# Tile shapes on TensorE and the planned order in a two-layer memory-attention kernel: 64x64 tiles for all 64-row products, 32-column quarters where they fit, an order from a slot table

## The chip, the core and the metric

The kernel runs on one core of a Trainium2 chip. The metric is the device time of one execution in microseconds; lower is better. The kernel before took 1589.48 us, the median of five runs between 1587.12 and 1594.11.

Engines are called as the profile calls them: PE is TensorE's matmul, PEld its weight load, DVE is VectorE, ACT ScalarE, POOL GpSimd, SP the queue that issues most DMAs. A matmul `MM(out, lhsT, rhs)` loads `lhsT` (rows x columns) into the array and streams `rhs` through it; "128x32" below is a tile of 128 rows and 32 columns of the array, and four such tiles can work at once, as can two of 64x128 or four of 64x64.

## The reference, cut to what matters

```
x = A_x                                   # 2048 positions, 448 wide, bf16
x = x + A(layernorm(x), mem0, ...)        # layer 0: attention with a recurrent memory
x = x + B(layernorm(x), ...)              # gated feed-forward, width 1792
x = x + A(layernorm(x), mem0, ...)        # layer 1, same weights
x = x + B(layernorm(x), ...)

def A(x, mem, Wq, Wk, Wv, Wo):            # 16 heads of 256
    for s in range(64):                   # segments of 32 positions
        h = concat([mem, x[segment s]])   # 8 + 32 = 40 rows
        q, k, v = h Wq, h Wk, h Wv
        p = softmax(masked(q k^T / 16))
        o = (p v) Wo
        mem, out[segment s] = o[:8], o[8:]

def B(x):  return (relu(x Wg) * (x Wu)) Wd
```

The memory of segment s+1 comes out of segment s, so the 64 segments of a layer are a chain.

## The kernel before, in words

**Folded weights.** A setup of some 67 us loads the weights and multiplies each head's Wq with its Wk (into `M`, and `M3` for the last 64 of the 448 rows) and Wv with Wo (into `N`). The 448-wide contraction is cut into three chunks of 128 rows (`c` or `kt` 0 to 2) and one of 64 rows (3). `NO = 56` output chunks of 128 stand for 16 heads of 448.

**Steps.** The two layers run in one loop of 68 steps; in step t, layer 0 works on segment t and layer 1 on segment t-4 (`LAG`). Up to step 3 there is only layer 0, in the last four only layer 1; between them a product of 40 rows a layer streams 80 columns. One step queues these operations (method, and tile shape on PE):

- `t_block` (L821): T = M^T h, 56 chunks in three blocks. A 64-row part (`first`) of pairs of chunks, two 64x128 tiles at once, then `rest`: three 128x128 matmuls of 80 columns a chunk. The last block has one unit and no pairs; it uses 128 rows throughout. Copies to `TTm` and `TTs` follow.
- `s_mem` (L890) and its softmax on DVE and ACT; `p_t_mem` (L961), a transpose; `u_mem` (L977), U = h^T p for the memory rows, in 64x128 tiles for three chunks and 64x64 for the last; `un_mem` (L990), U N in 128x32 tiles, four at once, 14 deep; its result is split into `hi` and `lo`; `m_t` (L1008) and, in the next step, `m_nat` (L1028) pick the new memory rows from them. This is the chain from step to step.
- `s_seg` (L912) and its softmax, `seg_pt` (L951, a transposing DMA from `Ps` to `PTs`), `u_seg` (L1059): the same for the 32 positions, off the chain; U products in 64x128 tiles for c < 3, 64x64 for c = 3.
- every second step: `un` (L1101), value sums over 56 chunks of 448 columns, for even p in 128x64 tiles, two at once, for odd p in 128x128; `ln_b`; `b_layer` (L1134), gate and up in a 64-row part (64x128 tiles, two at once) and a 128-row part, then down (`b_down` from L1166); `ln_a` of a later pair.

**The order.** No engine runs in the order above. `_Order.run` (L273) is a planner on the host: a list scheduler with a cost for each operation (`mm` L736, `dcost` L712, `acost`, `hop`), which at each turn takes, for the engine that can start earliest, the ready operation of highest priority. The priority is the longest path to the end plus a bias by the operation's name and step (`BIAS`, `bias_keys`). An operation has a `mode`, its tile shape (0: 128x128, 1: 64x128, 2: 128x32, 3: 64x64, 6: 128x64); `mode2` is the shape that it ends in. A change of mode costs 95 in the planner, and `stay` is a bonus for keeping it. Eight PSUM banks (`POOLS`) are handed out in planned order. Every engine then runs its list strictly in that order and waits on semaphores. All matmuls are issued by `_Sched.pe` (L117; the matmul itself is line 128 in the profile), all copies by `cp` (L725).

## Time and profile before

| What | Value |
|---|---|
| median of five runs | 1589.48 us (1587.12 to 1594.11) |
| the profiled execution | 1587.12 us, of which the span from first to last instruction is 1585.2 |
| granted TensorE clock, mean | 0.996 |
| matmuls, weight loads | 30146 each |
| DVE, ACT instructions | 2303, 2649 |
| DMA share over the span | 12.5% of 16 engines on the main queue |
| instruction fetch for the largest queue | 3.88 MB |

How to read it: the page's part 1 gives busy time by engine. Matmuls are pipelined, so the length of one (200 ns for 80 columns) says when its result is out, and the distance between two starts says what it costs. Timeline rows merge like instructions that stand next to each other: start, time to the last end, engine, line, operation, output and inputs, shape (rows*columns of the weights, then partitions x moving elements) and count; in brackets the idle time of the engine before the row and what ended it. Waits rows have engine, line and what it waited for, with total us, times, and the longest.

### The profile page before, as it was taken

The page shows a single profiled execution, that of the slowest core. Times are in us where ns is not written, and L with a number is a line of the kernel's source. Part 1 is how long each engine was busy: PE and PEld are TensorE (multiplying, and loading weights), DVE is VectorE, ACT ScalarE, POOL GpSimd, SP SyncE. Part 2 cuts the span into 40 slices and gives each one's busy share as a digit, 9 for nine tenths or more (in the row PEclk, how much of TensorE's full clock was granted, in tenths as well). Part 3 has the DMA queues.
Part 4 walks back from the last instruction along what each step waited for, and adds up shares of the span by engine and source line. Part 5 has one row for each costly group of instructions (what it writes and reads, how often), then busy time and mean ns, then how long its engine had stood idle before and what let it go on. Part 6 is the DMA issues. An engine that isn't in the chain of part 4 may idle for free.

```text
span 1585.2 us, 67069 instructions
## 1 busy us (share of the span) xinstructions
PE 1512.4 (95%) x30146; PEld 1082.9 (68%) x30146; DVE 869.7 (55%) x2303; ACT 861.5 (54%) x2649; POOL 111.1 (7%) x259
## 2 busy tenths in 40 slices
PE   5989999999999999999999999999999999999998
PEld 2456677767766776676767767776777677666775
DVE  6544546565554646555564655555465655556464
ACT  5735655555554565655555555555455465545443
POOL 4000000000000000000000000000000000000000
PEclk9999999999999999999999999999999999999999
DMA  9830000001000101010010001001000000000010
GB/s 216 224 80 18 18 9 19 19 18 15 15 19 11 23 15 19 19 15 15 18 20 11 19 19 16 17 16 19 11 19 19 19 15 18 14 14 19 13 21 13
DMA packets 128653, 45.04 MB, mean 28 GB/s; under 512 B 117480, under 2 KB 127472, under 8 KB 128368
## 3 DMA queue, kind: packets, MB, share of 16 engines
q1 hardware_dynamic: 128016, 40.52, 12.5%
q8 instruction: 237, 3.88, 1.1%
q14 instruction: 48, 0.39, 0.1%
q10 hardware_dynamic: 352, 0.24, 0.1%
HBM read 10.33 MB, written 1.84 MB: 8 GB/s over the span
## 4 chain that ended last, share of the span: by engine, by line
PE 86%; DVE 7%; DMA 3%; ACT 2%; issue 2%; POOL 0%; DVEq 0%; ACTq 0%; POOLq 0%
PE b L128 86%; DMA PTs<-Ps 2%; DVE lo L1006 1%; ACT hi L1005 1%; DVE stat L762 1%; DVE big L732 1%; DVE xn L769 1%; DVE ys L1185 1%; DVE XA L1177 1%; DVE UTm L732 1%; ACT stat L764 0%; ACT big L731 0%; DVE hT L732 0%; DMA xAT<-xn 0%; DVE seln L602 0%
## 5 line engine op out<-in xcount | busy, mean ns | idle before, releaser
L128 PE MATMUL b<-hT,Mw 128*128 128x80 bf16 (+1 forms) x11424 | 440.4, 200 | 9.3 <-DVE hT L732 5.5
L128 PEld LDWEIGHTS b<-hT,Mw 128*128 128x128 bf16 x11424 | 419.0, 100 | 34.5 <-DVE hT L732 14.9
L731 ACT ACTIVATE TTs<-b 128x320 bf16<-128x320 f32 (+5 forms) x698 | 297.3, 426 | 29.2 <-PE b L128 28.2
L128 PE MATMUL b<-Nw,big 128*64 128x448 bf16 (+1 forms) x1936 | 308.5, 355 | 0.2 <-ACT big L731 0.2
L731 ACT ACTIVATE TTm<-b 128x80 bf16<-128x80 f32 (+5 forms) x698 | 162.6, 233 | 159.3 <-PE b L128 156.2
L128 PE MATMUL b<-xBT,big 128*128 128x128 bf16 (+3 forms) x3920 | 199.4, 214 | 1.0 <-DMA xBT<-xn 0.6
L128 PEld LDWEIGHTS b<-Nw,big 128*64 128x64 bf16 (+1 forms) x1936 | 127.3, 104 | 106.0 <-issue 11.5
L128 PE MATMUL b<-Nw,UTm 128*32 128x448 bf16 x3752 | 191.0, 355 | 6.0 <-DVE UTm L732 4.9
L128 PEld LDWEIGHTS b<-xBT,big 128*128 128x128 bf16 (+1 forms) x3920 | 177.5, 97 | 19.0 <-ACT PTm L731 10.0
L128 PEld LDWEIGHTS b<-Nw,UTm 128*32 128x32 bf16 x3752 | 97.6, 97 | 95.9 <-ACT UTm L731 14.1
L731 ACT ACTIVATE big<-b 128x512 bf16<-128x512 f32 (+1 forms) x259 | 128.9, 567 | 35.4 <-PE b L128 35.1
L128 PE MATMUL b<-hT,M 64*128 64x80 bf16 (+3 forms) x3808 | 140.7, 197 | 2.7 <-DVE M L732 1.0
L732 DVE CAST TTm<-b 64x64 bf16<-64x64 f32 (+4 forms) x186 | 40.1, 216 | 163.9 <-PE b L128 161.8
L732 POOL COPY hK<-xn 32x448 bf16<-32x448 bf16 x136 | 75.0, 551 | 717.6 <-DVE xn L769 711.1
L128 PEld LDWEIGHTS b<-hT,M 64*128 64x128 bf16 (+1 forms) x3808 | 105.6, 97 | 22.5 <-DVE hT L732 7.7
L731 ACT ACTIVATE UTm<-b 128x448 bf16<-128x448 f32 (+2 forms) x129 | 70.3, 546 | 65.4 <-PE b L128 65.0
L732 DVE CAST UTm<-b 128x448 bf16<-128x448 f32 (+2 forms) x122 | 73.3, 621 | 56.0 <-PE b L128 54.0
L732 DVE CAST TTs<-b 64x256 bf16<-64x256 f32 (+4 forms) x186 | 73.2, 394 | 55.2 <-PE b L128 55.1
L1161 ACT ACTIVATE gT<-b 128x512 bf16<-128x512 f32 (+2 forms) x128 | 69.0, 539 | 53.4 <-PE b L128 53.3
L1162 DVE TENSOR_TENSOR hB<-gT,b 128x512 bf16<-128x512 bf16 (+2 forms) x128 | 78.4, 613 | 34.7 <-PE b L128 29.4
L128 PE MATMUL b<-big,hB 128*128 128x448 bf16 (+1 forms) x490 | 97.1, 354 | 0.0
L904 DVE TENSOR_REDUCE stat<-b 128x2 f32<-128x80 f32 (+1 forms) x67 | 15.7, 234 | 145.8 <-PE b L128 145.8
(111 smaller groups left out, 1615.1 us busy)
## 6 DMA issues: line engine op xcount, KB each, us to landing
big<-in_A_Wo_dram SPq DMA_DIRECT2D x3, 896.0 KB, 5.7
out_dram<-ys SPq DMA_DIRECT2D x32, 56.0 KB, 1.9
big<-in_B_W_down_dram SPq DMA_DIRECT2D x1, 1568.0 KB, 6.9
XA<-in_A_x_dram SPq DMA_DIRECT2D x28, 56.0 KB, 2.2
big<-in_B_W_up_dram SPq DMA_DIRECT2D x1, 1344.0 KB, 6.8
big<-in_B_W_gate_dram SPq DMA_DIRECT2D x1, 1344.0 KB, 11.3
PTs<-Ps SPq DMA_TRANSPOSE x67, 2.5
Nw<-in_A_Wo_dram SPq DMA_DIRECT2D x1, 896.0 KB, 6.4
```

What stands on the lines that cost most here:

```text
L128: ins = E.matmul(out, lhsT=lhsT, rhs=rhs, **kw)
L731: return E.activation(out(), src(), ACT.Copy)
L732: return E.tensor_copy(out(), src())
L762: S.dve(lambda E: E.bn_stats(st[:, so:so + 6], x), D, rd, [(key, 0)])
L769: S.dve(lambda E, a=a, b=b, src=src: E.tensor_scalar(S.xn[:, i, a:b], src, st[:, so + 6:so + 7], st[:, so + 8:so + 9], op0=ALU.subtract, o ...
L904: S.dve(lambda E: E.tensor_reduce(st[:, 32:32 + nl], src(), AX.X, ALU.max), n, C.res(), [("sm", 0)])
L1005: S.act(lambda E: E.activation(S.hi[:, :], C.b()[:, 0:D], ACT.Copy), D, C.res(), [("hi",)])
L1006: S.dve(lambda E: E.tensor_tensor(S.lo[:, :], C.b()[:, 0:D], S.hi[:, :], ALU.subtract), D, C.res() + [("hi",)], [("lo",)])
L1161: S.act(lambda E, g=g, R=R, n=n: E.activation(S.gT[:, g, 0:n], R[0].b()[:, 0:n], ACT.Relu), n, R[0].res(), [("gT", g)])
L1162: S.dve(lambda E, g=g, R=R, n=n, fcs=fcs: E.tensor_tensor(S.hB[:, fcs[0]:fcs[-1] + 1, 0:w], S.gT[:, g, 0:n].rearrange("p (a b) -> p a b", ...
L1177: S.dve(lambda E: E.tensor_tensor(S.XA[64:128, q % 4, :], O.b()[0:64, 0:D], S.XB[0:64, p % 2, :], ALU.add), D, O.res(half=(0,)) + xb, [("X ...
L1185: S.dve(lambda E: E.tensor_tensor(S.ys[64:128, p % 2, :], O.b()[64:128, 0:D], S.XB[64:128, p % 2, :], ALU.add), D, O.res(half=(1,)) + xb, ...
```

## The change

1. **64x64 tiles.** In `t_block` and `b_layer`, `first` issues four matmuls of 64 rows and 64 columns where it had two of 64 rows and 128 columns. `u_mms` does the same for c < 3. All these operations have mode 3; mode 1 is gone, and so is `mode2`.
2. **Quarters.** `un` for even p and the 64-row `b_down` issue 128x32 tiles (mode 2) in place of 128x64. `m_t`, `m_nat`, `un` for odd p and the full `b_down` get `alt=2`: when the planner has mode 2 at that point, each of their matmuls is issued as four of 32 columns (`quarters`), else as before.
3. **The order.** `BIAS` is replaced, and for PE operations of the steps a table `SLOT` (172 entries, by name, number and t % 4) with `PERIOD` gives the key; other operations get theirs from their successors. Choosing on PE, the planner adds 95 to the start of an operation in another mode; the window for choosing is 108 where it was 60.
4. **Costs in the planner** for DVE, ACT and POOL operations and for hops between engines are changed; they alter no instruction, only the order.

```diff
+PERIOD = 86000.0
+SLOT = {
+    "t_block0f.0@0": 15263, "t_block0r.0@0": 9584, "t_block0r.1@0": -78435, "t_block0r.2@0": -78572,
...
 def bias_keys(o):
     if not o.cat:
-        return [""]
-    phase = "a" if o.t < LAG else "z" if o.t >= NSEG else str(o.t % 4)
-    return [o.cat + ("" if o.kind == "pe" else "+"), o.cat + "@" + phase]
+        return []
+    if o.kind != "pe":
+        return [o.cat + o.sub + "+"]
+    return [o.cat + "@a"] if o.t < LAG else [o.cat + "@z"] if o.t >= NSEG else []
...
-        return 90.0 if b == "pe" else 35.0
+        return 35.0 if b != "pe" else 140.0 if a == "act" else 95.0
...
+            if o.slot in SLOT:
+                o.key = SLOT[o.slot] + PERIOD * (o.t // 4)
+            else:
+                lat = self.LAT[o.eng[0]] if o.lat is None else o.lat
+                o.key = min([q.key - (0.0 if o.kind == q.kind == "pe" else lat + 60.0) for q in o.succs], default=1e9) - min(o.cost.values())
+            o.key += sum(BIAS.get(k, 0.0) for k in bias_keys(o))
+            o.prio = -o.key
...
-                t0 = min(x[0] for x in lst)
-                lim = max(f, t0) + (60.0 if e == "pe" else 40.0)
+                sw = {o: 95.0 if e == "pe" and mode not in (o.mode, o.alt) else 0.0 for _, o in lst}
+                lim = max(f, min(x + sw[o] for x, o in lst)) + (BIAS.get("win", 60.0) if e == "pe" else 40.0)
...
             if e == "pe":
-                mode = o.mode2
+                if o.alt is not None and o.alt == mode:
+                    o.mode = mode
+                if o.mode != mode:
+                    c += 95.0
+                mode = o.mode
...
-                self.sc.pe(o.fn(), res(o.rd), res(o.wr))
+                mms = o.fn()
+                self.sc.pe(_Kernel.quarters(mms) if o.alt is not None and o.mode == 2 else mms, res(o.rd), res(o.wr))
...
-        return 150.0 + n / 0.96 / speed
+        return 156.0 + n / 0.96 if speed == 1 else 280.0 + 0.26 * n
...
+    def quarters(mms):
+
+        return [(out[32 * i:32 * i + 32], lhsT[:, 32 * i:32 * i + 32], rhs, kw) for out, lhsT, rhs, kw in mms for i in range(4)]
...
 # t_block, first():
-                    for x in (a, b):
+                    for o, x in ((0, a), (0, b), (1, a), (1, b)):
                         c, u0, m = units[x]
                         side, slot = S.PLACE[16 * c + u0 + j]
-                        h = slice(64 * side, 64 * side + 64)
-                        out.append(MM(R[x].b()[:, j * n:j * n + n], S.M3[h, slot, :], mov(3, h), start=(j == 0), stop=False))
+                        h, g = slice(64 * side, 64 * side + 64), slice(64 * o, 64 * o + 64)
+                        out.append(MM(R[x].b()[g, j * n:j * n + n], S.M3[h, slot, g], mov(3, h), start=(j == 0), stop=False))
...
 # u_mms:
-            return [MM(ps[:, 0:16 * w], S.hK[r, pp, s, c * 128:c * 128 + 128], PT[r, 0:16 * w], start=True, stop=True)]
+            return [MM(ps[64 * o:64 * o + 64, 0:16 * w], S.hK[r, pp, s, c * 128 + 64 * o:c * 128 + 64 * o + 64], PT[r, 0:16 * w], start=True, stop=True)
+                    for o in range(2)]
...
 # un, even p:
-                S.mm(lambda k=k: [MM(O.b()[64 * (o % 2):64 * (o % 2) + 64, 0:D], S.U[:, o, 32 * u[0]:32 * u[0] + 64], S.N[:, o, :], start=(o < 2), stop=(o >= NO - 2))
-                                  for o in range(k, k + 4)], 2 * S.pitch(D), [("U", i, k // 16) for i in u], O.res(), mode=6)
+                S.mm(lambda k=k: [MM(O.b()[64 * (o % 2) + 32 * i:64 * (o % 2) + 32 * i + 32, 0:D], S.U[:, o, 32 * u[i]:32 * u[i] + 32], S.N[:, o, :],
+                                     start=(o < 2), stop=(o >= NO - 2)) for o in range(k, k + 4) for i in range(2)],
+                     2 * S.pitch(D), [("U", i, k // 16) for i in u], O.res(), mode=2)
...
 # b_layer, first():
-                return [MM(R[x].b()[:, i * w:i * w + w], S.W3[64 * x:64 * x + 64, fc * 128:fc * 128 + 128], S.xBT[64 * x:64 * x + 64, 3, r],
-                           start=(i == 0), stop=False) for _, fcs, R in units for i, fc in enumerate(fcs) for x in range(2)]
+                return [MM(R[x].b()[64 * o:64 * o + 64, i * w:i * w + w], S.W3[64 * x:64 * x + 64, fc * 128 + 64 * o:fc * 128 + 64 * o + 64],
+                           S.xBT[64 * x:64 * x + 64, 3, r], start=(i == 0), stop=False)
+                        for _, fcs, R in units for i, fc in enumerate(fcs) for o in range(2) for x in range(2)]
```

Not shown: `m_t`, `m_nat`, `un` and `b_down` calls with `alt=2`, the 128x32 form of the short `b_down`, and names (`sub`) that tell operations apart in the table.

## The prediction

> **What bounds the kernel now.** First the page's busy times: which engine is full?

> ```profile
> span 1585.2 us, 67069 instructions
> PE 1512.4 (95%) x30146; PEld 1082.9 (68%) x30146; DVE 869.7 (55%) x2303; ACT 861.5 (54%) x2649; POOL 111.1 (7%) x259
> PE 86%; DVE 7%; DMA 3%; ACT 2%; issue 2%; POOL 0%; DVEq 0%; ACTq 0%; POOLq 0%
> ```

> PE is full, and the chain that ended last is 86% PE. DVE and ACT are half empty, so the change counts by what it does to PE. A busy share of 95% doesn't say what PE does with the time, so I took the timeline. The score products of TTm show that the program repeats every four steps (both layers of two positions): 90.8 us, such as this stretch (PE, PEld, DVE, ACT, POOL busy, clock, DMA):

> ```profile
> 607.10:697.90 90.80, 88.63 (x1778) 64.67 (x1776) 50.41 (x129) 50.43 (x155) 5.74 (x14) 1.00 0.10 17
> ```

> Then PE's own timeline inside one step (start, length, tile shape rows*columns, moving elements, count):

> ```profile
> 717.52 0.30 PE L128 MATMUL b<-PTs,hK 40*64 40x256 bf16 x4 [0.72 <-DVE big L732]
> 717.75 0.57 PE L128 MATMUL b<-Nw,big 128*64 128x448 bf16 x4
> 718.25 0.18 PE L128 MATMUL b<-selm,hi 128*128 128x16 bf16 x1
> ...
> 718.93 2.08 PE L128 MATMUL b<-Nw,big 128*64 128x448 bf16 x20
> 721.06 0.71 PE L128 MATMUL b<-hT,M 64*128 64x80 bf16 x30
> 721.70 0.28 PE L128 MATMUL b<-hT,Mw 128*128 128x80 bf16 x3
> ...
> 722.57 3.39 PE L128 MATMUL b<-hT,Mw 128*128 128x80 bf16 x90
> 725.89 0.53 PE L128 MATMUL b<-hT,M 64*128 64x80 bf16 x20
> 726.36 0.32 PE L128 MATMUL b<-hT,Mw 128*128 128x80 bf16 x4
> ```

> Read start to start, not lengths, which overlap. 30 matmuls of 64x80 (15 pairs, two row halves at once) take 721.70-721.06 = 0.64 us; 20 (10 pairs) take 0.47. The difference, 0.17 for five pairs, is 0.035 us a pair; what remains, 0.64 - 15x0.036 = 0.10 us, is paid once, where the tile shape changes. A full 128x80 matmul costs the same 0.036 (90 in 3.32 us, one change among them). **So a change of tile shape costs PE about 0.1 us**, and nothing else in these rows is slack.

> One period's pure streaming, from pitches read this way (0.036 for 80 columns, 0.056 for 128, 0.189 for 448, 0.216 for 512, 0.025 for 40 or fewer): T 4x(174+25)x0.036 = 28.7; scores 4x40x0.025 = 4.0; memory chain (transpose, U, selection, m_nat) 3.3; un_mem 4x14x0.19 = 10.6; U of the segment 3.0; value sums (28 pairs + 56)x0.189 = 15.9; gate/up 2x(14+84)x0.056 = 11.0; down 2x14x0.189 = 5.3. Sum 81.8 us. Over eight periods (607.1 to 1333.8) the timeline has 448 changes of shape, 56 a period; at 0.096 on average 5.4 us. The remaining 90.8-81.8-5.4 = **3.6 us are waits**, of which the waits view names 18 us in eight periods (waits over 150 ns only):

> ```profile
> PE b L128 <- DVE big L732: 5.7, 8, 0.7
> PE b L128 <- DVE lo L1006: 4.1, 7, 0.7
> PE b L128 <- DVE hT L732: 3.3, 8, 0.7
> PE b L128 <- DVE UTm L732: 2.6, 8, 0.3
> PE b L128 <- DMA PTs<-Ps: 2.1, 6, 0.7
> PE b L128 <- ACT big L731: 0.4, 2, 0.2
> ```

> All are short, eight in eight periods: the same places each time, set by the planned order.

> **The change, part by part.**

> *64x64 tiles* (T's 64-row parts, U, gate/up first). A pair becomes four matmuls of half the columns that stream together. Streaming saves nothing: 25 groups of 80 moving columns replace 25 pairs. What goes is a shape: U products change from 64x128 to 64x64 within themselves (48 times in eight periods), and all 64-row work can now stand side by side.

> The unknown is a long train of 64x64 groups; the trace has only single groups of four. Such a group at 717.52 took 0.23 us for 256 columns (0.107 of streaming), 0.02 to 0.03 above the 0.1 of a change; two pairs of 128*64 at 717.75 took 0.50 against 2x0.189+0.10, again 0.02. That is a 64-column load with nothing to hide it, about 25 ns. It isn't paid per pair: the ten pairs at 718.93 took 2.13 against 1.99 + 0.02, and PE waited for hT besides. Bounds for a group of 80 columns: 36 ns (the load lies under the previous group's 33 ns of streaming) to 61 (each pays its load). I take 36, plus 0.02 once a run. Removal of the cover is rival 3.

> [...] The rows above show 25 ns, and the measurement decides.

> Also the instructions: T gains 50 matmuls and 50 loads a step, U 12, gate/up 14, the even value sums 14. In T's groups eight instructions must start in 36 ns. The fastest lasting row is 30 matmuls of 64x40 at 101.41, 15 pairs in 0.48 us with a change: 25 ns for four instructions, 6.2 each, so a group would be 50. Bounds 36 to 50; single groups of eight begin within 13 ns, so I take 36 and keep 50 as rival 2.

> *32-column quarters.* Even value sums and the short down become 128x32 always; odd value sums, down, m_t and m_nat take that shape where PE is already in it. Pitch: 56 of 128x32 (un_mem) stand at 14 groups in 2.66 us, 0.19, the full matmul's 0.189. Cost nothing, up to 0.001 a group (0.1 us a period). m_t's eight matmuls of 16 moving columns become eight groups; 25 ns each, as now, to 50 (eight instructions at the 6.2 above), 0.8 us a period; I take 25, since 16 columns stream in less than the 40 of that row. Gain: changes between 128x64, 128x32 and 128x128.

> *Changes left.* Relabelling the shapes along the present order, 56 a period become 47. The new planner counts the change in when an operation is ready and keys each PE operation apart, so the order is new. The dependences of a step need T's first part (64), its rest (128), the second pair (64, 128), scores and transpose (128), U (64), un_mem to m_nat (32): six changes, 24 a period, if fillers fit. They can: behind un_mem wait hi, lo and hT, and value sums and down (5.3 us a step) are of its shape; behind the scores, the softmax waits for gate/up's main part and the segment's scores, all 128. Bounds 24 to 47; eight PSUM banks, six of them taken by T's first block, won't let every filler in. I take 30: 30x0.1 = 3.0, with 12 exposed 64-column loads (7 now) included.

> *Waits.* The new order moves copies on DVE and ACT and the transposing DMAs on SP past each other too; each waits in order behind what stands before it. Bounds: 0.9 us a period (three quarters gone) to 3.6 (none), and more in rival 4. The value sums and gate/up, 27 us a period of matmuls whose inputs are old, can stand in those places. I take half, 1.8. DVE and ACT stay at 55% and hide the rest; planner cost numbers change no instruction.

> **Sum.** 81.8+3.0+1.8 = 86.6 against 90.8: 4.2 us a period. The steps run from 67.6 to the end, 16.5 periods: 69 us. The setup keeps its shapes. The profiled execution took 1587.1 (span 1585.2 and 1.9 around it), so 1518; the median of the five runs is 2.4 above that execution, so **1520 us**. The range of this case alone is 1495 to 1545.

> **Rivals.**
> 1. The order gives little, only the relabelling: 47x0.1+3.6 puts the period at 90.2, 10 us less, 1579; with 40 changes and 3.2 of waits 89.0, 30 less, 1560. I put it at 1565. For it: the order was bound by banks and dependences before too. Against: six changes are needed, 14 stand there.
> 2. Instruction supply holds T's groups at 50 ns: 14 ns x25x67 = 23 us given back, 1543. For it: no row shows eight in 36 ns lastingly.
> 3. **Slower.** Every 64x64 group pays its 25 ns load: 25x67 of T, some 460 of gate/up, 400 of U, 2535x25 = 63 us. With the full gain of the order it is no change (1583); with relabelling alone 1640. It decides from 27 ns a group at the full gain, 4 at rival 1's.
> 4. No change: stalls in the new order, such as PE waiting for PTs (2.5 us from issue to landing), take a further 1 us a step, 67 us.

> **Chances.** Forecast 0.60, rival 1 0.15, rival 2 0.11, rival 3 0.08 (all slower), rival 4 0.06. Faster 0.86, same 0.06, slower 0.08, where 0.3% (4.8 us) is about what a measurement can tell. The range takes in the forecast's own, rivals 2 and 1 up to the relabelling bound: 1495 to 1578. The low end is 24 changes and 0.9 of waits, 85.3 a period, 91 us.

> **What would show it.** The period between score products: 86 to 87 us. 64*64 rows of 64x80 in runs of 60 and 40 that take 0.64 and 0.47 us start to start, as the pairs do now; 0.85 us for 60 is rival 2, over 1.0 rival 3. No 64*128 rows, 128*64 ones in the setup alone; un in 128*32 at 0.19 a group. About 30 changes of shape a period; 44 or more is rival 1. A wait for PTs, big or lo on PE above 1 us in each step would make the prediction wrong.

## The result, and the profile after

The changed kernel took 1586.28 us (median of 39 runs, 1582.88 to 1593.51), the kernel before 1590.55 in 65 runs beside them: ratio 0.9973, interval 0.9965 to 0.998. So 4 us were gained where 69 were forecast. The profiled execution took 1588.40 us, a span of 1586.5. (The slot table has 175 entries, not 172 as the text ahead says.)

The page of the changed kernel: busy times, then the queue that fetches PE's instructions (in the kernel before that row reads 237 packets, 3.88 MB).

```profile
span 1586.5 us, 82606 instructions
PE 1509.5 (95%) x37849; PEld 1109.9 (70%) x37849; DVE 878.1 (55%) x2316; ACT 864.7 (55%) x2636; POOL 111.3 (7%) x259
...
q8 instruction: 298, 4.88, 1.3%
```

PE is as full as before with 26% more matmuls. The same stretches of four steps (length, busy PE, PEld, DVE, ACT, POOL, clock, DMA):

```profile
597.60:687.10 89.50, 87.95 (x2221) 65.86 (x2219) 50.19 (x127) 50.82 (x155) 5.74 (x14) 1.00 0.11 18
687.10:777.10 90.00, 88.30 (x2219) 65.77 (x2218) 50.52 (x127) 50.93 (x155) 5.79 (x14) 1.00 0.09 18
```

Over eight periods (597.6 to 1318.9) one lasts 89.4 to 91.6 us, 90.2 on average, not 86.6. In PE's timeline of one step the shapes are what the change says, and T's groups can be priced:

```profile
608.12 0.73 PE L128 MATMUL b<-hT,M 64*64 64x80 bf16 x60
608.78 2.97 PE L128 MATMUL b<-hT,Mw 128*128 128x80 bf16 x78
...
614.48 0.55 PE L128 MATMUL b<-hT,M 64*64 64x80 bf16 x40 [0.54 <-ACT TTs L773]
614.97 2.33 PE L128 MATMUL b<-hT,Mw 128*128 128x80 bf16 x60
```

Start to start, 60 take 0.66 us and 40 take 0.49: five groups of four in 0.17 to 0.18, 0.036 a group, as forecast; 0.02 more a run than the pairs. So the tiles stream as they should. What is new stands in the waits of PE, here over the whole run, first of the kernel before:

```profile
PE b L128 <- DVE lo L1006: 13.1, 18, 1.5
PE b L128 <- DVE big L732: 10.0, 14, 0.7
...
PE b L128 <- issue: 7.0, 5, 3.2
...
PE b L128 <- DVE UTm L732: 4.9, 15, 0.3
PE b L128 <- DMA PTs<-Ps: 2.6, 8, 0.7
```

and of the changed one:

```profile
PE b L128 <- issue: 17.1, 29, 1.8
PE b L128 <- DVE lo L1061: 12.8, 17, 1.5
PE b L128 <- DVE xn L816: 9.6, 1, 9.6
PE b L128 <- DMA PTs<-Ps: 6.0, 7, 2.1
PE b L128 <- DMA ys<-in_A_mem_dram: 5.7, 1, 5.7
PE b L128 <- ACT TTs L773: 5.0, 10, 0.5
PE b L128 <- DVE Em L958: 2.8, 12, 0.2
```

"issue" is a wait in which the engine waited for nothing that the profile shows. It was 7.0 us in 5 places, it is 17.1 in 29, and many of the places are odd ones. 5.9 us of it stand in the middle of T's 128x128 train, with no semaphore near:

```profile
698.73 1.78 PE L128 MATMUL b<-hT,Mw 128*128 128x80 bf16 x45
701.00 0.78 PE L128 MATMUL b<-hT,Mw 128*128 128x80 bf16 x17 [0.49 <-issue]
```

45 matmuls at 0.036 leave the last start at 700.31; the next is at 701.00, 0.66 us late. I numbered all of PE's instructions in the trace, weight loads, matmuls and the semaphore instructions between them, and looked at the number at which such a gap ends. In the changed kernel 33 of the 43 gaps without a semaphore that are over 150 ns longer than pitch and change, and 19.6 of their 21.8 us, stand at the same remainder by 256 (193): **PE stops at the end of a block of 256 instructions.** The fetch queue agrees, with one packet of 16 KB a block: 298 packets for 76306 instructions (298.1 blocks), and 237 for 60764 (237.4) in the kernel before.

From the starts of all matmuls I split PE's time: streaming, changes of shape (up to 0.1 us each), gaps at a semaphore, gaps at a block's end without one, and the rest (among it stretches of halved clock). All in us of the profiled execution. The border between streaming and rest is loose: with one fixed pitch for each shape streaming is equal in both kernels, and the rest takes what differs.

| | before | after |
|---|---|---|
| streaming | 1386.0 | 1392.6 |
| changes of shape | 93.8 (988) | 73.2 (774) |
| waits at a semaphore | 77.4 | 74.9 |
| stalls at block ends | 4.9 | 20.4 |
| rest | 12.6 | 15.4 |

### The profile page after: what moved, and what is told of

Read it like the earlier page. It is cut to its first block, busy times and chain, and to the rows that moved or that the text cites. A ratio compares the mean times of both kernels' runs of the same rounds, so it can differ in the third digit from the quotient of the medians.

```text
span 1586.5 us, 82606 instructions
## 1 busy us (share of the span) xinstructions
PE 1509.5 (95%) x37849; PEld 1109.9 (70%) x37849; DVE 878.1 (55%) x2316; ACT 864.7 (55%) x2636; POOL 111.3 (7%) x259
## 3 DMA queue, kind: packets, MB, share of 16 engines
q1 hardware_dynamic: 128016, 40.52, 12.5%
## 5 line engine op out<-in xcount | busy, mean ns | idle before, releaser
L128 PE MATMUL b<-hT,Mw 128*128 128x80 bf16 (+1 forms) x11424 | 442.8, 200 | 8.1 <-issue 7.1
L128 PEld LDWEIGHTS b<-hT,Mw 128*128 128x128 bf16 x11424 | 419.2, 100 | 26.2 <-issue 14.5
L773 ACT ACTIVATE TTs<-b 128x320 bf16<-128x320 f32 (+4 forms) x694 | 290.5, 421 | 4.9 <-PE b L128 3.6
L128 PE MATMUL b<-Nw,big 128*32 128x448 bf16 (+1 forms) x3504 | 291.2, 353 | 0.5 <-issue 0.3
L128 PEld LDWEIGHTS b<-Nw,big 128*32 128x32 bf16 (+1 forms) x3504 | 139.8, 97 | 99.5 <-issue 3.5
L128 PE MATMUL b<-xBT,big 128*128 128x128 bf16 (+3 forms) x4900 | 205.8, 214 | 3.1 <-issue 2.1
L128 PEld LDWEIGHTS b<-xBT,big 128*128 128x128 bf16 (+1 forms) x4900 | 185.3, 102 | 18.2 <-issue 8.6
L128 PE MATMUL b<-Nw,UTm 128*32 128x448 bf16 x3752 | 192.9, 357 | 1.5 <-ACT UTm L773 1.3
L128 PE MATMUL b<-hT,M 64*64 64x80 bf16 (+2 forms) x7208 | 149.2, 199 | 12.9 <-ACT TTs L773 5.0
L128 PEld LDWEIGHTS b<-Nw,UTm 128*32 128x32 bf16 x3752 | 100.5, 97 | 83.0 <-issue 12.3
L128 PEld LDWEIGHTS b<-hT,M 64*64 64x64 bf16 (+1 forms) x7208 | 113.3, 108 | 46.3 <-issue 23.5
L774 DVE CAST TTm<-b 64x64 bf16<-64x64 f32 (+5 forms) x188 | 41.4, 220 | 143.0 <-PE b L128 141.0
L774 DVE CAST big<-b 128x512 bf16<-128x512 f32 x144 | 82.3, 598 | 67.0 <-PE b L128 66.8
L773 ACT ACTIVATE UTm<-b 128x512 bf16<-128x512 f32 (+1 forms) x143 | 81.7, 574 | 38.3 <-PE b L128 38.3
L128 PE MATMUL b<-big,hB 128*128 128x448 bf16 (+1 forms) x574 | 99.9, 354 | 0.4 <-DVE hB L1228 0.3
L957 DVE TENSOR_REDUCE stat<-b 128x2 f32<-128x80 f32 (+1 forms) x67 | 15.9, 237 | 137.5 <-PE b L128 136.5
L128 PE MATMUL b<-PTs,hK 40*64 40x512 bf16 (+1 forms) x1024 | 82.7, 363 | 9.5 <-DMA PTs<-Ps 6.0
```

Source lines behind the costliest of these rows:

```text
L128: ins = E.matmul(out, lhsT=lhsT, rhs=rhs, **kw)
L773: return E.activation(out(), src(), ACT.Copy)
L774: return E.tensor_copy(out(), src())
L957: S.dve(lambda E: E.tensor_reduce(st[:, 32:32 + nl], src(), AX.X, ALU.max), n, C.res(), [("sm", 0)])
```

## The experiments

Theory F: instructions come in blocks of 256, and PE stalls at a block's end when it has gone through the block faster than the next one came; T's 64x64 groups make the dense blocks. Rivals: theory O, only the order's waits and changes of shape keep the gain small; theory S, the 64x64 shape itself makes the stalls. The order of each kernel stayed as its planner made it; only what a planned operation issues was edited, so each pair of experiments 1 to 5 differs in tiles alone. Each ratio is to the kernel before, run beside that set, with a 95% interval; differences between ratios of different sets are less sure.

**1. T in pairs of 64x128 again, order untouched (a_t).**

```diff
-                    for o, x in ((0, a), (0, b), (1, a), (1, b)):
+                    for x in (a, b):
...
-                        out.append(MM(R[x].b()[g, j * n:j * n + n], S.M3[h, slot, g], mov(3, h), start=(j == 0), stop=False))
+                        out.append(MM(R[x].b()[:, j * n:j * n + n], S.M3[h, slot, :], mov(3, h), start=(j == 0), stop=False))
```

> The changed kernel in its own order, but T's 64-row parts issued as pairs of 64x128 matmuls again: 3400 matmuls fewer (34449), 790 changes of tile shape where it had 774. Theory F (instruction fetch: PE's stream comes in blocks of 256 instructions, and PE stalls at a block's end when it went through the block faster than the next one came; T's 64x64 groups make the dense blocks): the 20 us of such stalls in the changed kernel fall to about 10, 16 changes cost 1.6 back, so 6 to 10 us faster than the changed kernel, ratio 0.991 to 0.994 to the kernel before. Theory O (only the order's waits and changes of shape keep the gain small, the 64x64 tiles stream freely): 1.6 us slower than the changed kernel, ratio 0.998.

Measured: 1570.28 us, ratio 0.9887 (0.9869 to 0.9906). Stalls at block ends fell from 20.4 to 4.9 us, 790 changes took 74.9. By the ratios it is 14 us under the changed kernel, by the profiled spans 16: 15.5 us of stalls and 3.4 of streaming, less 1.7 of changes and some 1 of waits and rest. The waits of PE in this run, to be read against those above:

```profile
PE b L128 <- DVE lo L1061: 10.9, 15, 1.5
PE b L128 <- DVE xn L816: 9.4, 1, 9.4
PE b L128 <- ACT TTs L773: 7.3, 13, 0.6
PE b L128 <- DMA PTs<-Ps: 7.1, 10, 1.4
PE b L128 <- DMA ys<-in_A_mem_dram: 5.8, 1, 5.8
PE b L128 <- issue: 4.0, 4, 2.2
```

"issue" is down to 4.0 us, with the semaphore waits about where they were. Theory O, which had this version slower, falls. The gain is larger than F forecast, since the stalls fell to the level of the kernel before and not to 10.

**2. Gate/up in pairs too (a_tb), then U as well (a_tbu).** The same edit in `b_layer`, then in `u_mms`; a_tbu is the new order, with quarters, on the old 64-row tiles.

```diff
 # a_tb: b_layer, first()
-                return [MM(R[x].b()[64 * o:64 * o + 64, i * w:i * w + w], S.W3[64 * x:64 * x + 64, fc * 128 + 64 * o:fc * 128 + 64 * o + 64],
-                           S.xBT[64 * x:64 * x + 64, 3, r], start=(i == 0), stop=False)
-                        for _, fcs, R in units for i, fc in enumerate(fcs) for o in range(2) for x in range(2)]
+                return [MM(R[x].b()[:, i * w:i * w + w], S.W3[64 * x:64 * x + 64, fc * 128:fc * 128 + 128], S.xBT[64 * x:64 * x + 64, 3, r],
+                           start=(i == 0), stop=False) for _, fcs, R in units for i, fc in enumerate(fcs) for x in range(2)]
...
 # a_tbu: u_mms
-            return [MM(ps[64 * o:64 * o + 64, 0:16 * w], S.hK[r, pp, s, c * 128 + 64 * o:c * 128 + 64 * o + 64], PT[r, 0:16 * w], start=True, stop=True)
-                    for o in range(2)]
+            return [MM(ps[:, 0:16 * w], S.hK[r, pp, s, c * 128:c * 128 + 128], PT[r, 0:16 * w], start=True, stop=True)]
```

> As before, but gate/up's 64-row part as pairs of 64x128 too: 33469 matmuls, 838 changes of shape. Theory F: stalls at block ends fall a little more, to about 8 us, but 64 changes more than the changed kernel cost 6.4 us, so 4 to 6 us faster than it, ratio 0.993 to 0.996, and slower than the run with T alone. Theory O: 6 us slower than the changed kernel, ratio 1.001.

> The changed kernel's order with all 64-row matmuls as in the kernel before (T, gate/up and U's first three chunks in 64x128, U's last in 64x64), the quarters kept: 32704 matmuls, 938 changes of shape. What the order alone is worth. At 0.1 us a change, 100 more than the run with T and gate/up undone (1571) make 10 us: 1581, ratio 0.995 to the kernel before. If changes lie partly beside waits, as 48 of them did that cost 0.8 us instead of 4.8 there: 1573 to 1577, ratio 0.991 to 0.994. Stalls at block ends stay at 4 to 5 us either way.

Measured: 1571.06, ratio 0.9892 (0.9874 to 0.9911), stalls 4.3 us; and 1578.15, ratio 0.9924 (0.9906 to 0.9941), stalls 4.3. In the first, 48 more changes took 4.5 us of PE and the semaphore waits fell by 4.8: they lay beside waits, and the time rose by 0.8, which the intervals can't tell from nothing. F's ratio (0.993 to 0.996) missed, since a_t had left nothing more of stalls to gain. In the second, 100 more cost 5 us by the ratios, from separate sets whose intervals just touch. So the order and the quarters alone are worth 12 us, U's 64x64 tiles some 5, gate/up's nothing that the intervals can tell, and T's take 14 back: 4 are left.

**3. The old order with the new tiles: 64x64 alone (b64), 32-column tiles alone (bquart), both (btiles).** The edits are those of the change, without table, modes or costs; quarters are issued where the last tile was 32 columns wide.

```diff
 # kernel before, emit(): bquart and btiles
+                mms = o.fn()
+                if narrow and o.cat in ("un", "b_down", "m_t", "m_nat") and mms[0][1].shape[1] == 128:
+                    mms = [(out[32 * i:32 * i + 32], w[:, 32 * i:32 * i + 32], rhs, kw) for out, w, rhs, kw in mms for i in range(4)]
+                narrow = mms[-1][1].shape[1] == 32
```

> The kernel before with its order untouched, only T's, U's and gate/up's 64-row matmuls issued in 64x64 tiles: 5145 matmuls more (35291), 886 changes of shape where it had 988. Theory O: 102 changes less save 10 us, ratio 0.994. Theory F: the stalls at block ends rise from 5 to some 15 us and take the saving back, ratio 0.998 to 1.001.

> The kernel before with its order untouched, only even value sums and the short down in 128x32 tiles, and odd value sums, down, m_t and m_nat in 32-column quarters where PE is already in that shape: 3146 matmuls more (33292), 934 changes of shape. Theory O: 54 changes less save 5 us, ratio 0.997. Theory F says nearly the same, since these matmuls stream 448 columns and make no dense block: stalls stay at 5 to 8 us, ratio 0.997 to 0.999. If the number of instructions alone counted, the stalls would rise to some 10 us and the ratio be 1.000.

> The kernel before in its own order with all new tiles (64x64 and 32-column quarters): 38437 matmuls, 832 changes of shape. What the tiles alone are worth. By the two halves measured apart (1.0072 and 0.9999) the ratio is about 1.007, stalls at block ends 15 us or a little more. If 156 changes less were worth their 15 us and more, below 1.000.

Measured: 1599.8, ratio 1.0072 (1.0053 to 1.0092); 1587.89, ratio 0.9999 (0.9986 to 1.0012); 1604.5, ratio 1.0089 (1.007 to 1.0108). Stalls at block ends: 15.1, 4.3 and 19.1 us. b64 has 10 us less of changes (83.7) and is slower by 11: 10 of stalls, 5 of streaming, 7 in the rest. The stalls are F's, the time lies outside both theories' ranges. That the rest grew I had not expected; three of its stretches of halved clock stand in the middle of the run, and its six runs were granted a clock of 0.987 to 0.991 where the 17 of the kernel before beside them had 0.989 to 0.996. bquart has no more stalls, as F says, but of its 5 us of changes nothing is left (3 more of streaming, 3 of semaphore waits, 4 of rest), so its ratio lies above F's. These sums are of single profiled executions; where they don't meet the medians, they stay open.

**4. Many instructions in T without the 64x64 shape (a_tsplit).** a_t with each 64x128 matmul of T issued as two of 40 columns.

```diff
-                        out.append(MM(R[x].b()[:, j * n:j * n + n], S.M3[h, slot, :], mov(3, h), start=(j == 0), stop=False))
-            return out
+                        out.append((j, x, h, slot))
+            return [MM(R[x].b()[:, j * n + KEYS * i:j * n + KEYS * i + KEYS], S.M3[h, slot, :], S.hT[h, pp, 3, l0 + i, s, 0:KEYS], start=(j == 0 and i == 0), stop=False)
+                    for k in range(0, len(out), 2) for i in range(l1 - l0) for j, x, h, slot in out[k:k + 2]]
```

> As the run with T's 64-row parts in 64x128 pairs (1570), but each of these matmuls issued as two of 40 columns: 37449 matmuls, about the changed kernel's number, without its 64x64 tiles in T. Both theories put 14 ns a pair of such matmuls on it, since 40 columns start every 25 ns: 25x67x14 ns = 23 us. Theory F: the number of instructions in T makes the stalls, so those at block ends rise from 5 to 12 to 20 us, a little less than in the changed kernel because the matmuls come slower; 1600 to 1608. Theory S (the 64x64 shape itself makes the stalls): they stay at 5, and the time is 1593.

Measured: 1592.14, ratio 1.0019 (1.0005 to 1.0034). Streaming rose by 19.7 us to 1408.9, stalls at block ends from 4.9 to 9.7 us in 18 places. The time is theory S's (1593) and not F's; the stalls, on which the two differ, are neither's. T's rows (idle time, then what ended it) in the changed kernel, in a_t, and two of a_tsplit:

```profile
L128 PE MATMUL b<-hT,Mw 128*128 128x80 bf16 x10080 | 402.2, 202 | 6.9 <-issue 5.9 <-ACT hT L773 0.3
...
L128 PE MATMUL b<-hT,Mw 128*128 128x80 bf16 x10080 | 400.0, 202 | 1.5 <-issue 0.5 <-ACT hT L773 0.3
...
L128 PE MATMUL b<-hT,Mw 128*128 128x80 bf16 x10080 | 402.7, 203 | 3.6 <-issue 2.6 <-ACT hT L773 0.3
L128 PE MATMUL b<-hT,M 64*128 64x40 bf16 x6400 | 103.7, 177 | 10.0 <-ACT TTs L773 3.1 <-ACT M L773 2.5 <-ACT hT L773 2.1
```

T's 128x128 row has 5.9 us of issue in the changed kernel, 0.5 in a_t and 2.6 in a_tsplit. So more instructions bring stalls without the 64x64 shape, which speaks against S, but fewer than F's 12 to 20: spread over more streaming, the blocks are less dense. If the fetch holds PE, what counts is the time that a block lasts. I measured it for all blocks of the thirteen profiled kernels, without the stall at its end:

| a block's 256 instructions last | blocks | then a stall | us lost |
|---|---|---|---|
| under 3.0 us | 57 | 43 | 39.7 |
| 3.0 to 3.3 | 129 | 54 | 28.2 |
| 3.3 to 3.6 | 157 | 47 | 26.4 |
| 3.6 to 4.0 | 312 | 20 | 9.1 |
| 4.0 to 4.5 | 570 | 8 | 3.8 |
| over 4.5 | 2342 | 19 | 6.4 |

The shorter the block, the likelier the stall. Of blocks under 3.6 us the kernel before has 10, the changed one 54, a_t 11, a_tsplit 44, b64 36. The mechanism is seen in the fetch packets, one a block in order of time: in the stalled blocks of the changed kernel the packet mostly starts 0.4 to 1.8 us after PE entered the block, and PE goes on 2.3 to 2.9 us after that start. The block before the gap shown above was entered at 696.88 and lasted 3.43 us; its packet started at 698.39, and PE went on at 701.00, 2.61 us later. And in all 3567 blocks of the thirteen kernels, whatever their tile shapes, PE never left a block sooner than 2.18 us after the start of its packet. This floor holds in every shape, so the 64x64 shape isn't needed to explain the stalls. T's 128x128 train alone takes 256 instructions x 18 ns = 4.6 us, which is slow enough (19 stalls in 2342 blocks over 4.5 us); with 60 or 40 matmuls of the 64x64 kind in the block (120 or 80 instructions in 0.55 or 0.36 us), or with scores (12.5 ns an instruction), it isn't: by the same sum such blocks last an estimated 3.0, 3.5 and 3.2 us.

**5. The quarters left out (a_noq, a_t_noq).** `self.sc.pe(mms, ...)` in place of `quarters(mms)`, in the changed kernel and in a_t.

> The changed kernel with odd value sums, down, m_t and m_nat always in full 128x128 tiles, order untouched: 1410 matmuls fewer (36439), 822 changes of shape where it had 774. Theory F: these stream 448 columns, so the stalls at block ends change little, 18 to 20 us; 48 changes cost at most 4.8 us: 1586 to 1591, ratio 0.998 to 1.001.

> T's 64-row parts in 64x128 pairs and no quarters of odd value sums, down, m_t and m_nat: 33039 matmuls, 838 changes of shape. Theory F: the stalls at block ends are at 5 us already and can't fall, and 48 changes more cost 1 to 5 us: 1571 to 1575, ratio 0.989 to 0.992. If fewer instructions pay by themselves, as leaving the quarters out of the changed kernel paid 4 us: 1566, ratio 0.986.

Measured: 1582.23, ratio 0.9948 (0.9932 to 0.9965), and 1566.54, ratio 0.984 (0.9812 to 0.9868). Theory F's figures missed in both, in the same direction; in the second the alternative, that fewer instructions pay by themselves (1566), came out. 48 more changes took 4 us of PE, and yet the ratio fell by 0.0025 (4 us) and by 0.0047 (7 us, between separate sets of runs). The stalls at block ends went from 20.4 to 11.0 and from 4.9 to 1.3 us. Value sums and m_nat, of 448 columns, make no dense block by themselves, but they are only 618 of the 1410 matmuls left out. The other 792 are m_t's, in 16 columns, which the expectations overlooked:

```profile
L128 PE MATMUL b<-selm,hi 128*32 128x16 bf16 x528 | 11.2, 171 | 3.8 <-DVE lo L1061 3.6
```

A run of 32 of these (`hi` and `lo`), 64 instructions, takes 0.20 to 0.25 us from start to start in the changed kernel, 3 to 4 ns an instruction, the densest stretch of all. On the old order they brought no stalls by themselves (bquart, 4.3 us). Leaving them out also moves where blocks end; which of the two did it I haven't separated. **The second is the fastest version run that keeps the recurrence**, faster than both kernels: 1.6% under the kernel before.

**6. Without the wait for hi and lo (a_nochain, a_t_nochain).** The kernels leave out the recurrence of the memory.

```diff
-... for i, x in enumerate((S.hi, S.lo))
+... for i, x in enumerate((S.N[:, 0, :], S.N[:, 1, :]))        # m_t and m_nat
+                rd = [r for r in o.rd if not (o.cat in ("m_t", "m_nat") and r[0] in ("hi", "lo"))]
```

> The changed kernel, order untouched, in which m_t and m_nat multiply two constant rows of N where they read hi and lo, so the new memory rows are not the reference's and PE no longer waits for hi and lo; all other instructions stay. Which waits keep the time. The trace of the changed kernel has 12.8 us of PE waiting for lo. Theory C (the chain from step to step sets the pace, so what is late there is lost): 10 to 15 us less, 1572 to 1576, ratio 0.989 to 0.992. Theory P (the waits are for PSUM banks and copies as much, and PE meets the next of them when one is taken away): under 6 us less, ratio 0.994 to 0.997.

> The same in the version with T's 64-row parts in 64x128 pairs (1570): m_t and m_nat read constants, no wait for hi and lo. Theory C: 1556 to 1560, ratio 0.980 to 0.983. Theory P: 1565 to 1569, ratio 0.986 to 0.988.

Measured: 1578.08, ratio 0.9918 (0.9886 to 0.995), and 1564.41, ratio 0.9824 (0.9794 to 0.9854). Both ratios lie in theory C's range (the medians 2 and 4 us above it), 9 and 10 us under the same versions with the chain. The waits of PE in the first:

```profile
PE b L128 <- issue: 11.9, 17, 2.0
PE b L128 <- DVE xn L817: 9.4, 1, 9.4
PE b L128 <- ACT hT L774: 8.6, 18, 1.9
PE b L128 <- DMA PTs<-Ps: 7.4, 8, 2.5
PE b L128 <- ACT TTs L774: 6.5, 12, 0.5
```

Of the 12.8 us for lo 2.5 are left in the trace, and 8.6 for hT stand there, 2.4 in the changed kernel: the copy of m_t's result, next in the same chain. Semaphore waits fell by only 4.3 us in all, from 74.9 to 70.6, and by 2.6 in the other: so in the trace a wait that is taken away comes back in good part at the next late thing. In the first run the stalls at block ends fell by 6.5 as well, which the experiment didn't aim at, so its time isn't a clean price of the chain. The time speaks for C, the waits partly for P; what of the waits the chain keeps stays open.

## Why the prediction was wrong, by its own steps

- What the sum lacks, by size: some 27 us of waits that stayed, 18 of changes that stayed, 15.5 of stalls, for which it had no term, and up to 7 of streaming.
- **Streaming** (81.8, unchanged): right within 0.4 us a period. T's groups cost 36 ns (60 matmuls in 0.66 us), the lower bound that was taken, and a run 0.02 us more than the pairs; that these 0.02 are an exposed load is the prediction's estimate, and no run shows the load's part in them. The upper bound of 61 ns, with a load paid in every group, didn't show.
- **Changes left** (30 a period): failed by size. The timeline has 44 (352 in eight periods), the number that was to mark rival 1. They fell by 2.4 us a period in the forecast and by 1.3 in the trace. The floor of six a step counted T's two blocks, U of memory and the chain, and let fillers in freely; in the trace the segment's U products stand in two or three separate runs a step (x4, x8, x12), and gate/up's in two runs more. That the eight PSUM banks force this is argued from the list of runs, not shown. And a change didn't always cost the time its 0.1 us: 48 of them took 4.5 us of PE and cost 0.8 in one pair of runs, where the semaphore waits fell by 4.8; 100 cost some 5 in another.
- **Waits** (half of 3.6 gone): failed, and by the most. The half was a choice between two bounds that no row bore out. Semaphore waits over the whole run fell by 2.5 us, not by 30. They moved: big and UTm went, TTs, Em and PTs came, lo stayed. Experiment 6 shows the same: a wait that is taken away comes back in good part as the next (lo fell by 10.3 us, all semaphore waits by 4.3). What in the order keeps the waits there no run shows.
- **Instructions** (36 ns taken, 50 kept as rival 2): the step that failed in its mechanism. The added matmuls were counted and the question was put, but to the wrong grain: eight instructions in 36 ns do start, lastingly (60 matmuls in 0.66 us). What PE lacks is the next 256, a term that the sum put at nothing. At 15.5 us more of stalls it is two thirds of the price that rival 2 set (23), by another mechanism, and undoing T's tiles alone gives 14 to 16 us back. The profile of before held the hint: 237 packets of 16 KB for 60764 instructions of PE, one each 256.
- The sum in the terms of the prediction: of 69 us, changes brought 21 where 39 were meant, semaphore waits 2.5 of 30; stalls took 15.5, streaming 6.6, the rest 2.8. Together 1.8 us longer, where the two profiled executions differ by 1.3; the medians differ by 4 the other way, since one execution lies 3.4 us under its median of 65 runs and the other 2.1 above its own. The granted clock goes with it: 0.996 in the first, where 41 other runs of the kernel before had 0.991 at the median, and 0.992 in the second.
- **One period times 16.5**: the sum took each period's gain for the whole run. The eight periods in the middle are 0.7 us shorter each, which would make 11 us, and stalls of 6.5 us in the eight are already in it. The first steps took that back: between 70 and 240 us of the span, waits, stalls and rest take some 33 us where they took 21, by the same split with the prediction's pitches. In that stretch 20.5 us ran at half the clock where 6.8 did.
- The order: worth 12 us with the quarters (a_tbu), at the low end of rival 1's 10 to 30. On the old order the same tiles cost 14 us. Tiles and order can't be added up: U's and gate/up's 64x64 tiles gain a further 6 us in the new order.

## What to carry to other kernels

When a change splits matmuls into smaller tiles at equal streaming, work out how long PE takes for each 256 of its instructions: in these kernels 144 of the 343 blocks under 3.6 us led to stalls, 27 of the 2912 over 4 us. A gap marked "issue" inside a train, with no semaphore, is worth numbering by instruction. And don't price a saved wait or a saved change at its full length while other waits stand beside it (here 48 changes cost 0.8 us where their price was 4.8): measure order and tiles apart, by issuing the old tiles in the new order and the new tiles in the old one.
